# Moving eleven weight-conversion turns of a fused attention, gated-MLP and mixer kernel to earlier batches, with a new order in the last batch

## The chip, the cores and the metric

The kernel runs on one core of a Trainium2 chip. Its time is the device time of one execution in microseconds (us), taken as the median over several runs. One execution was also recorded by the hardware profiler, and all rows quoted below come from that one.

The engines have short names: PE is TensorE (matmuls), DVE is VectorE, ACT is ScalarE, POOL is GpSimd, and SP is SyncE, which here only issues DMA transfers.

## What is computed

Three layers follow one another, for a batch of 8, with 576 rows and 512 columns, all in float32:

```python
# attention: softmax of q over d, of k over s; no s x s matrix
q_s = softmax(q, axis=-1)
k_s = softmax(k, axis=2)
kv  = einsum('bhsd,bhse->bhde', k_s, v)
x   = einsum('bhsd,bhde->bhse', q_s, kv)          # heads joined to 512 columns
# gated MLP
u, v = split(gelu(x @ w_in))                       # 512 columns each
v_n  = (v - mean) / sqrt(var + 1e-6) * g_ln        # layer norm of v
v_s  = einsum('ts,bsd->btd', w_sg, v_n) + b_sg     # mixes the 576 rows
y    = x + (u * v_s) @ w_out
# mixer
u    = y + ((y^T @ U) @ V)^T                       # rank 32
out  = u + relu(u @ w_ch1) @ w_ch2                 # 512 -> 2048 -> 512
```

## The kernel before, in words

**Precision.** Nearly every matmul is made of three products of a high and a low part (`prod`, matmuls at L52). So each operand is split first: a rounding copy to the high part (L61, on ACT) and a subtraction that leaves the low part (L55, on DVE or POOL).

**Two phases.** The first phase is a loop over the eight batches. In this text b counts from 0, so b = 1 to 6 are batches 2 to 7 and b = 7 is the last. The 576 rows are four tiles of 128 and a short one of 64. The second phase is the channel MLP, over all batches at once in groups of rows: a long run of matmuls named `mm` that read weights `wu` back from a DRAM scratch `wd`.

**One batch has five stages.** In the V stage, `emit_Vh` makes the v half of `x @ w_in` tile by tile (`pv`), ACT applies the GELU, and DVE takes the row statistics (`stats`, L644 to L646). `emit_ln` then scales by the norm on ACT (L657) and splits. Beside it run the transposes, the rank-32 products and `emit_PV` of the batch before; `emit_PV` is the matmul `pw`, added into `yt` on DVE. In the U stage, `emit_Uh(b, f)` for f = 0 to 3 makes the u half (`pu`), and ACT turns each `pu` into `ut` with a GELU (L688). Beside it the next batch's softmax begins: DVE subtracts the row maximum (`q_sub`, `k_sub`), ACT takes exponentials (`q_exp` L483, `k_exp` L464). In the S stage, `emit_S(b, f)` makes the row mix (`pS`), DVE gates it (L708 and a multiplication by `ut`; that of f = 2 is done by POOL, by the table `GATES_POOL`), and `split_G` splits it into `gh` and `gl`. The y stage has the next batch's `kv` and transposed q (`pt`, split into `qh` on ACT and `ql` on DVE) and `emit_y(b, c)` (`py`), evicted into `yt` on DVE. The x stage makes the next `x`. The last batch has no next one; in its place the first products of the channel MLP (`pm`) run, on parts of u prepared by the steps of `prep` (`us`, `uh`, `ul`; loaded from the DRAM copy `u2d`).

**PSUM.** The tiles `pw`, `pu`, `pS`, `pt` of q and `py` share one pool of three buffers (tag `big`, `ps2`). Each takes the buffer of the third one before it, and so waits for whoever reads that one last. `pS` of f = 2 takes over from `pu` of f = 3, and waits for ACT's `ut` of f = 3. `py` of c = 1 takes over from the first `pt`, and waits for its `ql`. The last `pt` of q takes over from `py` of c = 1, and waits for its `yt`.

**Conversion turns.** The weights of the channel MLP are also split and summed before they are used. That work is cut into turns. The table `TURNS` lays 127 of them into the batches (per batch and stage, a string per slot; each `T` is a turn), `STEP_TURNS` 16 into the last batch's steps with `pm`, and `GROUP_TURNS` the rest into the second phase. `more(1)` does one turn: load the raw block (SP, L213, `stg`), clamp it (POOL, L171), take its rounding exponent (ACT, L177), merge (DVE, L183 and L184), add factor sums, write the high copy (`chw`, ACT, L61) and the low part (`chw`, POOL or DVE, L55), store to `wd` (SP, L384).

**What sets the order.** PE follows program order. DVE follows program order in the whole loop, since the loop body sits in `in_order(dve)`. The order on ACT, POOL and SP is chosen by the scheduler, by when it reckons each operation's input to be ready. Changing the place of an operation on DVE can therefore change the order on ACT too.

ACT holds one set of functions at a time. Going from exponentials to GELU or back takes an instruction of its own, `ACT_TABLE_LOAD`.

Of the kernel before, what the change touches and what calls it, by code (L numbers as in the profile page):

```python
# [22 lines left out]
def fused_kernel(tc, q, k, v, w_in, g_ln, w_sgT, b_sg, w_out, U, V, w_ch1, w_ch2, outT):  # L23
# [295 lines left out]
    GATES_POOL = ((), (2,), (2,), (2,), (2,), (2,), (2,), (2,))  # L319
# [3 lines left out]
    class Block(Conv):  # L323
# [14 lines left out]
        def high(self):  # L338
            pass
# [380 lines left out]
    y_t = {}  # L720

    def emit_y(b, c):
# [94 lines left out]
    def u_parts(g, kc):  # L817
# [6 lines left out]
        else:  # L824
            parts = [wrk.tile([P, F], F32, tag=x, name="us") for x in ("vh2", "vl2", "vh3", "vl3")]
# [10 lines left out]
    def u_first():  # L836
# [4 lines left out]
        for kc in range(2):  # L841
# [28 lines left out]
            if kc:  # L870
# [8 lines left out]
                high(5, u22)  # L879
                yield  # L880
                rest(5, u22)
                yield
                rest(4, u21)
                yield
# [331 lines left out]
    def in_order(*engines):  # L1216
# [107 lines left out]
    for b in range(B):  # L1324
# [13 lines left out]
        for t in range(NT + 1):  # L1338
            emit_Vh(b, t)
            if nxt:  # L1340
                with behind(dve):
                    for t2 in Q_MAX[b > 0][t]:
                        q_max(nxt, t2)
                    for _ in range(FOLDS[b > 0][t]):
                        next(fold)
            if t < NT:
                stats(b, t)
            slot(TURNS[b][0][t])
            if t > 0:
                emit_ln(b, t - 1)  # L1350
            if t == NT:
                stats(b, t)
            if b > 0:
                for t2 in ((2,), (3, 4), (), (), ())[t]:
                    emit_yT(b - 1, t2)
# [262 lines left out]
```

## Time and profile before

| | us |
|---|---|
| median of 3 runs | 1293.57 (1293.42 to 1298.71) |
| the profiled execution, its own time | 1292.16 |
| its span, first to last instruction | 1290.4 |
| PE busy | 1261.8 (98%) |
| DVE busy | 969.8 (75%) |
| ACT busy | 653.3 (51%) |
| POOL busy | 324.3 (25%) |
| mean granted TensorE clock | 0.989 of full speed |

The time is 1.8 us longer than the span, for what lies before the first and after the last instruction. Busy shares are averages over the program; stretches differ, and the stretch is what a change of a stage must be read from. In a row of a timeline, the first number is the start, the second the time from the start of the first to the end of the last of the instructions joined in it; the bracket at its end is how long the engine sat idle before and who ended that.

### The profile page before, as it was taken

What the parts mean: (1) busy time and instruction counts of PE and PEld (TensorE: products, weight loads), DVE (VectorE), ACT (ScalarE), POOL (GpSimd) and SP (SyncE); (2) the same over time, 40 slices, a digit from 0 to 9 for tenths busy, and PEclk for the clock granted to TensorE, in tenths of its full rate; (3) what the DMA queues carried; (4) which work ended last, traced back from release to release, by engine and by line L of the source; (5) the groups of instructions that cost most, each with busy time, mean ns of one, the idle gap of its engine ahead of it and who ended that gap; (6) DMA issues with size and microseconds to landing.
All of it is one profiled execution on the core that took longest, in us unless ns stands there. A gap on an engine that the chain in (4) does not pass through costs nothing.

```text
span 1290.4 us, 20684 instructions
## 1 busy us (share of the span) xinstructions
PE 1261.8 (98%) x7628; PEld 1142.8 (89%) x7628; DVE 969.8 (75%) x1406; ACT 653.3 (51%) x998; POOL 324.3 (25%) x421
## 2 busy tenths in 40 slices
PE   6999999999999999999999999999999999999998
PEld 5798999999998989797887888888888889999998
DVE  6898889797988888788769943597347953694485
ACT  5756667675757576754563512443224522451342
POOL 4734152623333334663630202000200002000000
PEclk8899999999999999999999999999999999999999
DMA  8515161715343352568998676678766788898786
GB/s 271 167 55 167 51 207 51 235 51 167 99 158 117 113 170 76 195 202 284 397 346 295 213 257 235 220 246 281 259 189 224 256 286 303 274 314 302 256 297 212
DMA packets 135909, 274.17 MB, mean 212 GB/s; under 512 B 15232, under 2 KB 56704, under 8 KB 135808
## 3 DMA queue, kind: packets, MB, share of 16 engines
q1 hardware_dynamic: 135808, 272.84, 64.0%
q8 instruction: 61, 1.00, 0.3%
q14 instruction: 40, 0.33, 0.1%
HBM read 224.56 MB, written 48.23 MB: 211 GB/s over the span
## 4 chain that ended last, share of the span: by engine, by line
PE 82%; DVE 8%; DMA 4%; ACT 3%; issue 1%; POOL 1%; SPq 1%; DVEq 0%; POOLq 0%; ACTq 0%
PE mm L52 51%; PE pS L52 8%; PE py L52 6%; PE pv L52 5%; PE pu L52 5%; PE px L52 1%; PE pk L52 1%; PE pt L553 1%; PE pt L741 1%; PE pp L52 1%; DVE bst L644 1%; DVE sh L654 1%; DMA wu<-wd 1%; DVE yt L55 1%; PE pm L52 1%
## 5 line engine op out<-in xcount | busy, mean ns | idle before, releaser
L52 PE MATMUL mm<-oh,wu 128*128 128x512 f32 (+1 forms) x1120 | 320.5, 367 | 1.2 <-DMA wu<-wd 1.2
L52 PE MATMUL mm<-uh,wu 128*128 128x512 f32 (+1 forms) x1064 | 303.4, 366 | 0.0
L52 PEld LDWEIGHTS mm<-oh,wu 128*128 128x128 f32 x1120 | 207.1, 188 | 27.6 <-ACT oh L61 1.6
L52 PEld LDWEIGHTS mm<-uh,wu 128*128 128x128 f32 x1064 | 196.6, 188 | 24.1 <-issue 0.2
L52 PE MATMUL mm<-ol,wu 128*128 128x512 f32 (+1 forms) x560 | 205.5, 367 | 0.0
L61 ACT ACTIVATE oh<-h 128x1024 fp32r<-128x1024 f32 (+1 forms) x140 | 135.2, 973 | 125.3 <-PE mm L52 104.6
L52 PE MATMUL mm<-ul,wu 128*128 128x512 f32 (+1 forms) x532 | 194.7, 366 | 0.0
L55 DVE TENSOR_TENSOR ol<-h,oh 128x1024 fp32r<-128x1024 f32 (+1 forms) x140 | 156.4, 1121 | 40.1 <-ACT oh L61 37.2
L55 POOL TENSOR_TENSOR ust<-ust 128x1024 f32<-128x1024 f32 (+1 forms) x16 | 36.3, 2278 | 384.5 <-DMA ust<-u2d 323.6
L55 DVE TENSOR_TENSOR h<-mm,u 128x1024 f32<-128x1024 f32 (+1 forms) x57 | 63.3, 1111 | 83.8 <-PE mm L52 83.8
L52 PEld LDWEIGHTS mm<-ol,wu 128*128 128x128 f32 x560 | 105.1, 188 | 13.2
L55 DVE TENSOR_TENSOR u<-mm,u 128x1024 f32<-128x1024 f32 (+1 forms) x53 | 58.9, 1111 | 73.2 <-PE mm L52 68.1
L52 PEld LDWEIGHTS mm<-ul,wu 128*128 128x128 f32 x532 | 99.9, 188 | 12.1
L55 POOL TENSOR_TENSOR chw<-f,chw 128x256 fp32r<-128x256 f32 x98 | 80.7, 836 | 97.6 <-ACT chw L61 87.6
L55 DVE TENSOR_TENSOR h<-h,h 128x1024 f32<-128x1024 f32 (+1 forms) x80 | 88.9, 1111 | 0.1
L1102 ACT ACTIVATE h<-mm 128x1024 f32<-128x1024 f32 (+1 forms) x19 | 17.8, 938 | 128.3 <-PE mm L52 128.3
L1093 ACT ACTIVATE h<-h 128x1024 f32<-128x1024 f32 (+1 forms) x60 | 58.1, 969 | 33.6 <-DVE h L55 33.6
L61 ACT ACTIVATE chw<-f 128x256 fp32r<-128x256 f32 x112 | 42.5, 411 | 63.6 <-DVE f L184 30.7
L61 ACT ACTIVATE u<-mm 128x1024 f32<-128x1024 f32 (+1 forms) x24 | 22.5, 936 | 96.3 <-PE mm L52 80.0
L171 POOL TENSOR_SCALAR stg<-stg 128x256 f32<-128x256 f32 (+1 forms) x88 | 44.3, 508 | 91.3 <-DMA stg<-in_w_ch_dram 50.4
L52 PE MATMUL pu<-xh,wih 128*128 128x288 f32 x256 | 57.9, 308 | 1.9 <-ACT wih L61 0.6
L52 PE MATMUL pu<-xh,wil 128*128 128x288 f32 x256 | 56.3, 301 | 1.8 <-DVE wil L55 1.8
(177 smaller groups left out, 2661.8 us busy)
## 6 DMA issues: line engine op xcount, KB each, us to landing
wu<-wd SPq DMA_DIRECT2D x280, 512.0 KB, 4.4
wd<-chw SPq DMA_DIRECT2D x112, 256.0 KB, 3.5
stg<-in_w_ch_dram SPq DMA_DIRECT2D x64, 256.0 KB, 3.5
u2d<-yt SPq DMA_DIRECT2D x32, 288.0 KB, 2.3
vt<-in_v_dram SPq DMA_DIRECT2D x32, 256.0 KB, 6.9
qt<-in_q_dram SPq DMA_DIRECT2D x7, 1024.0 KB, 8.2
kt<-in_k_dram SPq DMA_DIRECT2D x7, 1024.0 KB, 6.4
res<-u2d SPq DMA_DIRECT2D x12, 512.0 KB, 5.8
```

Of the source, the lines that this page charges most:

```text
L52: pe.matmul(out, lhsT, rhs, start=first, stop=last, skip_group_check=onto)
L55: return eng.tensor_tensor(out=out, in0=a, in1=b, op=op)
L61: return act.activation(out, src, AF.Copy)
L171: eng.tensor_scalar(out=hi, in0=hi, scalar1=F64_MOST, scalar2=-F64_MOST, op0=ALU.min, op1=ALU.max)
L553: pe.transpose(pt[:, t * P : (t + 1) * P], qt[:, t, c * P : (c + 1) * P], ident)
L644: dve.bn_stats(out=bst[0:n], in_=ge[0:n])
L654: dve.scalar_tensor_tensor(out=shift[0:n], in0=mv[0:n, 0:1], scalar=-1.0, in1=mv[0:n, 1:2], op0=ALU.mult, op1=ALU.mult)
L741: pe.transpose(pt[0:n, c * P : (c + 1) * P], y_t[b][:, c, t * P : t * P + n], ident)
L1093: act.activation(h, h, AF.Relu)
L1102: act.activation(h_out(j, 11, n), bank, AF.Relu)
```

## The change

It has four parts.

1. `TURNS`: 11 turns leave the last batch (29 to 18) and go to b = 1 to 4. Within those batches further turns go from the y stage to the S stage: the S stages of b = 1, 2, 3, 4 had 7, 6, 8 and 6 turns and have 12, 12, 11 and 9; the y stages had 8, 10, 6 and 8 and have 7, 7, 7 and 8. The sum over the batches stays 127, and the steps and the second phase have the turns they had.
2. In b = 1 to 6, two `q_sub` are put between the scaling and the split of the short tile's norm. They were the first after it.
3. The last batch: `emit_PV` and the low-rank copy come ahead of `stats` in the V stage, the short tile's norm and the `prep` steps are placed anew, its S stage has no turns, all gate multiplications are on DVE, `emit_y` for c = 0 and 1 runs jointly (f = 0 to 2 of both, then f = 3 of both), one scratch buffer is another, and some slots come after the added products.
4. In the last batch ACT follows program order too, from the U stage to the end of the y stage.

```diff
-    GATES_POOL = ((), (2,), (2,), (2,), (2,), (2,), (2,), (2,))
+    GATES_POOL = ((), (2,), (2,), (2,), (2,), (2,), (2,), ())
...
-        py = ps2.tile([P, 2, 512], F32, tag="big", name="py")
-        cs = slice(c * P, (c + 1) * P)
-        for fc in range(NF):
-            prod(py, wo_h[:, fc, cs], wo_l[:, fc, cs], gh[:, fc], gl2[:, fc], fc == 0, fc == NF - 1)
+        cols = (c,) if b < B - 1 or c > 1 else (0, 1)
+        if c == cols[0]:
+            for x in cols:
+                py_t[x] = ps2.tile([P, 2, 512], F32, tag="big", name="py")
+            for fcs in (range(NF - 1), range(NF - 1, NF)):
+                for x in cols:
+                    cs = slice(x * P, (x + 1) * P)
+                    for fc in fcs:
+                        prod(py_t[x], wo_h[:, fc, cs], wo_l[:, fc, cs], gh[:, fc], gl2[:, fc], fc == 0, fc == NF - 1)
+        py = py_t.pop(c)
...
-        (('T', '', '', '', ''), ('', '', '', ''), ('T', 'T', 'TTT', 'TT'), ('TT', 'TTTT', 'TTW', ''), ('', '', '', '', '')),
+        (('T', '', '', '', ''), ('', '', '', ''), ('TTT', 'TTTT', 'TTTT', 'T'), ('TT', 'TTT', 'TTW', ''), ('', '', '', '', '')),
...
-        (('TTT', 'TT', 'TT', 'T', 'TT'), ('TT', 'T', 'T', 'TTT'), ('TT', 'T', 'TT', ''), ('TTT', 'TT', 'PT', 'T')),
+        (('TTT', 'TT', 'TT', '', 'TTT'), ('T', 'T', '', ''), ('', '', '', ''), ('TT', 'TT', 'PT', 'T')),
...
+        else:
+            for t in range(NT + 1):
+                emit_Vh(b, t)
+                if t == 2:
+                    for t2 in range(NT + 1):
+                        emit_U(b - 1, t2)
+                for c in ((), (), (), (0, 1), (2, 3))[t]:
+                    emit_PV(b - 1, c)
                 stats(b, t)
+                if t >= NT - 1:
+                    emit_ln(b, t - 1)
+                slot(TURNS[b][0][t])
+                if 0 < t < NT - 1:
+                    emit_ln(b, t - 1)
...
+            acts = in_order(act)
+            acts.__enter__()
...
                 if b and nxt:
-                    emit_ln(b, NT)
+                    ln_scale(b, NT)
+                    for t in Q_SUB[1][0]:
+                        q_sub(nxt, t)
+                    ln_split(b, NT)
```

Three places where the order of instructions changes follow. The first is ACT in the U stage of b = 5, from the scaling of the short tile (L657, 64 rows) to the last `ut`. `qt` and `kt` are the next batch's exponentials, `vh` of 64 rows is the short tile's high copy. Before:

```order
L657 ACTIVATE ge<-ge,sh,mv 64x512
L61 ACTIVATE vh_5089<-ge 64x512
L688 ACTIVATE ut<-pu 128x576 x2
L483 ACT_TABLE_LOAD
L483 ACTIVATE qt<-qt 128x512 x4
L688 ACT_TABLE_LOAD
L688 ACTIVATE ut<-pu 128x576
L483 ACT_TABLE_LOAD
L483 ACTIVATE qt<-qt 64x512
L464 ACTIVATE kt<-kt 128x512 x4
L688 ACT_TABLE_LOAD
L688 ACTIVATE ut<-pu 128x576
```

And now, from the table load behind the same scaling:

```order
L483 ACT_TABLE_LOAD
L483 ACTIVATE qt<-qt 128x512
L61 ACTIVATE vh_5149<-ge 64x512
L483 ACTIVATE qt<-qt 128x512
L688 ACT_TABLE_LOAD
L688 ACTIVATE ut<-pu 128x576 x2
L483 ACT_TABLE_LOAD
L483 ACTIVATE qt<-qt 128x512 x2
L483 ACTIVATE qt<-qt 64x512
L464 ACTIVATE kt<-kt 128x512
L688 ACT_TABLE_LOAD
L688 ACTIVATE ut<-pu 128x576
```

```order
L464 ACT_TABLE_LOAD
L464 ACTIVATE kt<-kt 128x512 x4
L61 ACTIVATE chw<-f_4732 128x256
L61 ACTIVATE chw<-f_4714 128x256
L688 ACT_TABLE_LOAD
L688 ACTIVATE ut<-pu 128x576
```

The first exponentials moved ahead of the first two `ut`: six table loads and all ten exponentials now come before the last `ut`, where four loads and nine exponentials stood. Each of b = 1 to 6 has this order; the two `chw` copies ahead of the last load are there in b = 5 only.

The second is DVE at the end of the S stage of b = 3, from the last gating (L708) to the first two `ql`. Before:

```order
L708 SCALAR_TENSOR_TENSOR gt<-pS,gl,bb 128x576
L55 TENSOR_TENSOR gt<-gt,ut 128x576
L55 TENSOR_TENSOR gl_3518<-gt,gh 128x576 x2
L183 TENSOR_SCALAR f_3650<-f_3650 128x256
L184 SCALAR_TENSOR_TENSOR f_3650<-stg,f_3650 128x256
L55 TENSOR_TENSOR ql<-pt,qh 128x576 x2
```

And now:

```order
L708 SCALAR_TENSOR_TENSOR gt<-pS,gl,bb 128x576
L55 TENSOR_TENSOR gt<-gt,ut 128x576
L55 TENSOR_TENSOR gl_3558<-gt,gh 128x576 x2
L55 TENSOR_TENSOR chw<-f_2994,chw 128x256
L183 TENSOR_SCALAR f_3692<-f_3692 128x256
L184 SCALAR_TENSOR_TENSOR f_3692<-stg,f_3692 128x256
L183 TENSOR_SCALAR f_3701<-f_3701 128x256
L184 SCALAR_TENSOR_TENSOR f_3701<-stg,f_3701 128x256
L55 TENSOR_TENSOR ql<-pt,qh 128x576 x2
```

One merge stood between `gl` and `ql`; now a low part and two merges do.

The third is DVE in the V stage of the last batch, from the low-rank copy `pst` to the first additions of `emit_PV`. Before:

```order
L55 TENSOR_TENSOR pst<-pp,pst 32x512
L644 BN_STATS bst<-ge 128x6
L645 BN_AGGR mv<-bst 128x2
L646 TENSOR_SCALAR mv<-mv 128x1
L183 TENSOR_SCALAR f_6710<-f_6710 128x256
L184 SCALAR_TENSOR_TENSOR f_6710<-stg,f_6710 128x256
L654 SCALAR_TENSOR_TENSOR sh<-mv 128x1
L55 TENSOR_TENSOR yt<-pw,yt 128x576 x2
```

And now:

```order
L55 TENSOR_TENSOR pst<-pp,pst 32x512
L644 BN_STATS bst<-ge 128x6
L645 BN_AGGR mv<-bst 128x2
L646 TENSOR_SCALAR mv<-mv 128x1
L183 TENSOR_SCALAR f_6707<-f_6707 128x256
L184 SCALAR_TENSOR_TENSOR f_6707<-stg,f_6707 128x256
L183 TENSOR_SCALAR f_6716<-f_6716 128x256
L184 SCALAR_TENSOR_TENSOR f_6716<-stg,f_6716 128x256
L654 SCALAR_TENSOR_TENSOR sh<-mv 128x1
L55 TENSOR_TENSOR yt<-pw,yt 128x576 x2
```

The statistics and the two merges that now follow `pst` stood just ahead of it before. The additions now stand ahead of the next tile's statistics and merge, which they followed.

## Rows read from the trace of the kernel before

**Rows 1.** The page, part 1: busy time, share and instructions of each engine.
```profile
PE 1261.8 (98%) x7628; PEld 1142.8 (89%) x7628; DVE 969.8 (75%) x1406; ACT 653.3 (51%) x998; POOL 324.3 (25%) x421
```

**Rows 2.** Windows by stage: us, busy time per engine, PEclk, DMA share, GB/s.
```profile
382.80:451.50 68.70, 68.49 (x532) 64.61 (x531) 59.96 (x110) 44.34 (x74) 24.19 (x36) 1.00 0.39 126
...
520.20:613.00 92.80, 88.87 (x540) 79.07 (x539) 76.85 (x129) 53.15 (x105) 50.01 (x63) 1.00 0.67 222
613.00:686.00 73.00, 71.82 (x317) 59.23 (x317) 52.34 (x64) 39.93 (x65) 35.33 (x49) 1.00 1.01 375
```

**Rows 3.** Timeline of ACT, U stage of b = 5: start, us, instruction, idle before.
```profile
409.64 0.82 ACT L657 ACTIVATE ge<-ge,sh,mv 64x512 f32<-64x512 f32 x1 [1.50 <-DVE sh L654]
...
411.70 1.20 ACT L688 ACTIVATE ut<-pu 128x576 f32<-128x576 f32 x2 [0.58 <-DMA u2d<-yt]
412.91 1.28 ACT L483 ACT_TABLE_LOAD   x1
414.21 2.19 ACT L483 ACTIVATE qt<-qt 128x512 f32<-128x512 f32 x4
...
423.70 0.65 ACT L688 ACTIVATE ut<-pu 128x576 f32<-128x576 f32 x1
...
426.21 0.71 ACT L61 ACTIVATE chw<-f 128x256 fp32r<-128x256 f32 x2
```

**Rows 4.** Timeline of PE, the same stretch: the start of `pS` for f = 2.
```profile
425.91 0.42 PE L52 MATMUL pS<-sg_h,vh 128*128 128x288 f32 x2
```

**Rows 5.** Timeline of DVE, S to y stage of b = 3.
```profile
293.91 1.65 DVE L55 TENSOR_TENSOR chw<-f,chw 128x256 fp32r<-128x256 f32 x1
...
296.13 0.42 DVE L55 TENSOR_TENSOR chw<-f,chw 128x256 fp32r<-128x256 f32 x1
...
299.32 1.64 DVE L55 TENSOR_TENSOR gl<-gt,gh 128x576 fp32r<-128x576 f32 x2
300.88 0.28 DVE L183 TENSOR_SCALAR f<-f 128x256 uint32<-128x256 uint32 x1
...
301.54 1.42 DVE L55 TENSOR_TENSOR ql<-pt,qh 128x576 fp32r<-128x576 f32 x2
```

**Rows 6.** Timeline of PE, the same stretch: the start of `py` for c = 1.
```profile
302.94 0.43 PE L52 MATMUL py<-gh,wo_h 128*128 128x288 f32 x2
```

**Rows 7.** Timelines of DVE, POOL and PE, y stage of b = 1.
```profile
169.01 0.76 DVE L55 TENSOR_TENSOR yt<-py,x 128x576 f32<-128x576 f32 x1 [1.41 <-PE py L52]
...
168.99 1.45 POOL L55 TENSOR_TENSOR chw<-f,chw 128x256 fp32r<-128x256 f32 x2
...
172.54 0.71 PE L553 MATMUL pt<-ident,qt 128*128 128x128 f32 x5
```

**Rows 8.** Timeline of PE in the last batch, V to U stage.
```profile
539.05 0.80 PE L52 MATMUL pw<-v_w,pst 128*128 128x288 f32 x4 [0.26 <-DVE pst L55]
...
541.55 0.43 PE L52 MATMUL pw<-v_w,pst 128*128 128x288 f32 x2
543.27 0.53 PE L52 MATMUL pw<-v_w,pst 128*128 128x288 f32 x2 [1.29 <-DVE yt L55]
543.94 0.54 PE L52 MATMUL pu<-xh,wih 128*128 128x288 f32 x2
...
547.85 0.53 PE L52 MATMUL pu<-xh,wih 128*128 128x288 f32 x2 [0.46 <-DVE yt L55]
```

**Rows 9.** Waits of PE from 519 to 690 us: total us, times, longest us.
```profile
PE pw L52 <- DVE yt L55: 1.7, 2, 1.3
PE mm L52 <- DMA wu<-wd: 1.2, 1, 1.2
PE pm L52 <- ACT h L1102: 0.8, 1, 0.8
PE py L52 <- DVE gl L55: 0.5, 1, 0.5
```

**Rows 10.** Timeline of ACT in the last batch: its third part of u.
```profile
550.89 0.64 ACT L61 ACTIVATE uh<-us 128x512 fp32r<-128x512 f32 x1 [0.63 <-DMA us<-u2d]
```

More of the change, by code (lines that the diff above doesn't have):

```diff
@@ L720, in fused_kernel @@
     y_t = {}
+    py_t = {}
     def emit_y(b, c):
@@ L824, in u_parts @@
         else:
-            parts = [wrk.tile([P, F], F32, tag=x, name="us") for x in ("vh2", "vl2", "vh3", "vl3")]
+            parts = [wrk.tile([P, F], F32, tag=x, name="us") for x in ("vh2", "vl2", "vh3", "vh4")]
         parts = [t[:, 0:n] for t in parts]
@@ L878, in u_first @@
                 tt(dve, u22, u22, u11, ALU.subtract)
-                high(5, u22)
-                yield
-                rest(5, u22)
                 yield
                 rest(4, u21)
+                yield
+                high(5, u22)
+                rest(5, u22)
                 yield
@@ L1337, in fused_kernel @@
             load_ahead()
[L1338 to L1346, printed above, removed]
-                stats(b, t)
[L1348 to L1353, printed above, removed]
+        if nxt:
+            for t in range(NT + 1):
+                emit_Vh(b, t)
+                if nxt:
+                    with behind(dve):
+                        for t2 in Q_MAX[b > 0][t]:
+                            q_max(nxt, t2)
+                        for _ in range(FOLDS[b > 0][t]):
+                            next(fold)
+                if t < NT:
+                    stats(b, t)
+                slot(TURNS[b][0][t])
+                if t > 0:
+                    emit_ln(b, t - 1)
+                if t == NT:
+                    stats(b, t)
+                if b > 0:
+                    for t2 in ((2,), (3, 4), (), (), ())[t]:
+                        emit_yT(b - 1, t2)
+                if t == 2 and b > 0:
+                    for t2 in range(NT + 1):
+                        emit_U(b - 1, t2)
+                if b > 0:
+                    for c in ((), (), (), (0, 1), (2, 3))[t]:
+                        emit_PV(b - 1, c)
+        else:
+            for t in range(NT + 1):
+                emit_Vh(b, t)
+                if t == 2:
+                    for t2 in range(NT + 1):
+                        emit_U(b - 1, t2)
+                for c in ((), (), (), (0, 1), (2, 3))[t]:
+                    emit_PV(b - 1, c)
+                stats(b, t)
+                if t >= NT - 1:
+                    emit_ln(b, t - 1)
+                slot(TURNS[b][0][t])
+                if 0 < t < NT - 1:
+                    emit_ln(b, t - 1)
                 for t2 in ((2,), (3, 4), (), (), ())[t]:
                     emit_yT(b - 1, t2)
-            if t == 2 and b > 0:
-                for t2 in range(NT + 1):
-                    emit_U(b - 1, t2)
-            if b > 0:
-                for c in ((), (), (), (0, 1), (2, 3))[t]:
-                    emit_PV(b - 1, c)
         spread_at = 2 if b else 3
@@ L1384, in fused_kernel @@
             if not nxt:
-                for _ in range((0, 3, 3, 3)[f]):
+                for _ in range((0, 1, 3, 3)[f]):
                     next(prep, None)
@@ L1403, in fused_kernel @@
             if nxt:
-                for t in Q_SUB[b > 0][f]:
+                for t in Q_SUB[b > 0][f] if b == 0 or f else ():
                     q_sub(nxt, t, pool if t in Q_SUB_POOL[b > 0] else dve)
@@ L1413, in fused_kernel @@
                         k_sub(nxt, t)
-            if not nxt and f == 1:
+            if not nxt and f == 2:
                 ln_split(b, NT)
@@ L1417, in fused_kernel @@
                 slot(TURNS[b][1][f])
-            if not nxt and f == 0:
+            if not nxt and f == 1:
                 ln_scale(b, NT)
@@ L1439, in fused_kernel @@
         for f in range(NF):
+            if not nxt:
+                for _ in range((5, 0, 0, 0)[f]):
+                    next(prep, None)
             emit_S(b, f)
@@ L1447, in fused_kernel @@
                     k_exp(nxt, ((0, 1, 2), (3, 4))[f])
-            if not nxt:
-                for _ in range((2, 0, 0, 0)[f]):
-                    next(prep, None)
             if f > 0:
@@ L1457, in fused_kernel @@
             with tc.issue_after(last['s'].ins):
-                for _ in range(2):
+                for _ in range(1):
                     next(prep, None)
@@ L1504, in step @@
                 after(s)
-                for _ in range((1, 0, 9, 0, 0, 0, 0)[s]):
+                for _ in range((1, 0, 0, 0, 0, 0, 0)[s]):
                     next(prep, None)
-                slot(STEP_TURNS[s])
+                if s < 4:
+                    slot(STEP_TURNS[s])
             pvl = ((), (), (), (), (0, 1), (2,), (3,))
@@ L1526, in fused_kernel @@
                 pvs(s)
-                for _ in range(2 if s == 1 else 0):
+                for _ in range((0, 2, 9, 0, 0, 0, 0)[s]):
                     next(prep, None)
+                if s >= 4:
+                    slot(STEP_TURNS[s])
         gate.clear()
```

2 lines of the change are left out of this document (added), and 5 rows, old and new, of the table TURNS.

## The prediction, made before the result was known

> **What bounds the kernel now.** I read the busy shares first [rows 1]: PE has 98%, the next engine 75%. A time can then only change where PE starts late, so the second view is the table of windows [rows 2]. In b = 5, which stands for b = 1 to 6 (six windows of 68.6 to 68.8 us), PE is busy 68.49 of 68.70 us: there is next to nothing to win in these batches, only to lose. The last batch has 3.9 us without PE in 92.8. The stretch behind it has 1.2 in 73, with the DMA engines full (share 1.01).
>
> The third view is PE's waits from 519 us on [rows 9]. Its four largest kinds are 4.2 us in five waits, and two more of 0.26 and 0.46 stand in the timeline [rows 8]: 4.9 in seven. A wait costs a little more than its length, because the pipeline fills again: a pair of these matmuls steps on by 0.27 (0.43 for a pair, less the 0.16 by which the pairs overlap), so after 541.55 the next was due at 541.82 and came at 543.27, 1.45 late for a wait of 1.29. With 0.16 for each of the seven, and 0.4 more at the pair after that (0.67 to 543.94 in place of 0.27 [rows 8]), **6.4 us is all that this change can win**: 0.49% of the time. What a measurement of this kernel can tell from no change is about 0.5%, or 6.47 us. So a measurable gain is nearly excluded before any part is costed. The question is what the parts lose.
>
> **Part 1, the two subtractions in the short tile's norm: a loss of 7.0.** The subtractions themselves only swap places on DVE. But they are done earlier, and so ACT's order turns over: exponentials now come ahead of the first two `ut`, and six table loads instead of four ahead of the last. I lay ACT's new order out with the old durations. In b = 5 the scaling of the short tile ends at 409.64 + 0.82 = 410.46 [rows 3]. Behind it stand:
> - six table loads of 1.28, with a gap of 0.02 each (412.91 + 1.28 to 414.21): 7.8;
> - ten exponentials at 2.19 / 4 = 0.55: 5.5;
> - the short tile's copy, at the price of one of two `ut` (1.20 less 0.65): 0.55;
> - four `ut`, 1.20 for two and 0.65 for each of the others: 2.5.
>
> That is 16.35, so the last `ut` ends at 426.8. It ended at 424.35 before (423.70 + 0.65). `pS` of f = 2 needs the buffer that it frees, and started at 425.91 [rows 4]: what was a slack of 1.5 becomes a wait of 0.9, and 0.15 of refill makes 1.05. The order and the durations repeat in b = 1 to 6, so six times 1.05 is 6.3. In b = 5 two high copies stand ahead of the last load besides, 0.71 [rows 3]. **Sum 7.0.** PE has no slack behind it in which this could come back. The wait of the first `ut` for a DMA (0.58 [rows 3]) doesn't add: the load that now comes first isn't held by it, and 0.58 is over by then. DVE's low part of the short tile waits for a later copy, some 1.8 us; that is work PE needs only at the end of the first `pS`, so it costs nothing while `pS` is itself late.
>
> Bounds of this part: at least 4, if unlike instructions overlap by half a microsecond more per batch than the sum has it; at most 9.5, if ACT also waits for DVE's subtractions 0.4 per batch.
>
> **Part 2, the added turns: a loss of 2.2.** Each adds a clamp, an exponent, a merge of 0.7 (300.88 to 301.54 [rows 5]), copies, lows and DMAs. DVE is busy 60 of 68.7 us and the DMA share is 0.39 [rows 2], so the engines have the room; only the place counts. SP's and POOL's queues get up to five turns more within an S stage; POOL is busy 24 of 68.7 and loses nothing but order.
> - In b = 3, a low part and a second merge come between `gl` and the first `ql`. A low part took 0.42 alone and 1.65 beside POOL [rows 5], which are DVE's bounds for it; I take 0.42 for want of a POOL operation there. With the merge that is 1.1. ACT's order too puts the last `gh` behind the first two `qh`, which wait for PE's transposes; I reckon that this holds `gl` back by 1.9: two copies go ahead of it, at a `ut`'s 0.6 each [rows 3], and the transposes that they wait for come with PE's own delay of 1.05, of which 0.7 tells (they were done a little before they were asked for). `ql` ended at 302.96 in pair, its first half at 302.25; `py` of c = 1 started at 302.94 [rows 6], a slack of 0.7. With 3.0 more for `ql`, and 1.05 more for `py` by PE's own delay, 1.3 is left: **1.4** with the refill. Bounds 0 (if `gh` goes first in time after all) and 2.6 (the low part at its slow price).
> - In b = 1, three merges stand between the first and second `yt`, and their exponents on ACT are behind a `qh` and a POOL low part (1.45 for two [rows 7]). The second `yt` ended at 169.77; the last transposes, which need its buffer, started at 172.54 [rows 7], so 2.8 of slack. Three merges are 2.1, the POOL pair 1.45, two exponents 0.4 each (as half of the two copies of 0.71 [rows 3]): 4.4, against 2.8 of slack and 1.05 of PE's delay. That leaves 0.6, with refill **0.8**; bounds 0 and 1.7, as the exponents find POOL free or held up twice.
> - In b = 2 and b = 4 what comes between the same pairs is no more than one merge, which the slack of 0.7 and PE's delay cover: 0. Without this cover it would be 0.7 each at the most, which I leave to the range.
>
> **Part 3, the last batch: a gain of 4.2.** The copy `pst` and the additions of `emit_PV` stood on DVE behind statistics and merges. Now they stand ahead. PE's starts came late at four places there: 0.42 before 539.05 and 0.62 before 547.85 (their waits and refill), 1.45 before 543.27 and 0.4 before 543.94 [rows 8]: 2.9 together, which I count as won in full, since the engines that were waited for had other work in front that is now behind. The joint `emit_y` puts the first three f of c = 1 between the last gate and the first use of its `gl`: that wait of 0.5 [rows 9] goes, 0.7 with refill. Of the wait of `pm` for ACT (0.8) and the second of `pw` (0.4, the rest of 1.7 [rows 9]), which hang on work that starts earlier but stands in the same order, I count half: 0.6. The wait for `wu` (1.2 [rows 9]) stays: the DMA engines are full there [rows 2] and must move the same bytes. Bounds 2.5 and 5.5.
>
> **The sum.** 7.0 + 1.4 + 0.8 - 4.2 = +5.0. The profiled execution took 1292.16, and would take 1297.2; the median is 1.4 above the profiled one, so the time shown for the changed kernel should be 1293.57 + 5.0 = **1298.6**. By its own bounds it lies between 1294 and 1303.
>
> **What the Trainium skill says of it.** In this trace an exponential starts 0.02 us after a table load of 1.28 ends, and the load 0.01 after the `ut` before it [rows 3]: a switch costs 1.30 and no more. The Trainium skill, "ScalarE: Activation LUTs", section "What ACT_TABLE_LOAD costs", gives about 1283 ns for the load, which the trace has too, and a drain of about 1380 ns with it, 2.66 us for every switch. The trace here shows no such drain. By that rule the two added loads would cost 5.3 per batch and not 2.6, and the sum would be some 16 us higher.
>
> **The rivals.**
> - *The last batch gives nothing back* (slower). In the last batch ACT now keeps the written order, and two `uh`, which wait for the loads of u from DRAM, stand ahead of the second `ut`. `pS` of f = 0 needs that `ut`, and is due 2.9 us earlier than before, at about 554.6. The third such part was ready at 550.89 before [rows 10]; if ACT reaches the `ut` as that one ends, it is done at 552.2, with 2.4 to spare. The point from which this decides: loads that land over 2.4 us later than they did. For it: the DMA engines serve stores and weight loads in the same stretch. Against it: the turns there went away, 11 of them, and their transfers with them. Then the 2.9 are lost again: +7.9, **1301.5**.
> - *ACT isn't late* (faster, or none). If the last `ut` were done by 425.9, 0.9 earlier than my sum, part 1 would cost nothing but b = 5's copies, and part 2 nothing that isn't covered. Only the gain of part 3 is left: 1293.57 - 4.2 + 0.7, **1290**. For it: the sum has single gaps taken from other neighbours, and the wait is small against 16 us. [...]
> - *Both, and all of PE's waits go:* -6.4, **1287**. Against it: the wait for `wu`, on full DMA engines.
> - *A table load drains as well* (slower). If each of the two added loads held ACT for as long again as its 1.28 [rows 3], `pS` of f = 2 would wait 2.6 more in each of six batches: +15.4, **1314**. It is the mechanism of the Trainium skill's rule above. Against it: the gaps of 0.01 and 0.02.
>
> **How the numbers follow.** My forecast gets 0.62: it rests on ACT's order and on durations that repeat. The last batch giving nothing back gets 0.17, ACT not late 0.16, all waits gone 0.03, the drain 0.02. The range from **1290** to **1304** takes in the forecast with its bounds, the first rival with the upper bound of part 2, and the 1290 of the second; what it leaves out is half of the second, the two last ones, and the ends of the bounds: under 0.2. Slower by over 0.5% means above 1300.04: the first rival with 0.13 of its 0.17, the drain, and a fourth of the forecast, together 0.31. Faster by over 0.5% means below 1287.1: 0.03. The rest, 0.66, is within 0.5%. The forecast itself lies at +0.39%, on the slow side of no change.
>
> **What would show it.** In the changed profile's waits of PE, a line for `pS` released by ACT at L688, six times, about 1 us each and longest in b = 5; the windows of b = 1 to 6 each some 1.1 longer with the same busy PE time; a wait of `py` for DVE's `ql` in b = 3. In the last batch, no wait of `pw` for `yt`, and a stage shorter by 4. I am wrong if `pS` shows no wait for ACT, if the last batch isn't shorter, or if PE waits at another place for over 2 us.

## The result, and the profile after

| | before | changed |
|---|---|---|
| median of the runs, us | 1294.55 (1293.42 to 1298.71, 6 runs) | 1305.36 (1301.12 to 1306.31, 6 runs) |
| ratio, 95% interval | | 1.0072 (1.0052 to 1.0093) |
| profiled execution: span, us | 1290.4 | 1299.3 |

The change makes the kernel slower by 0.72%, some 9.3 us: the ratio is that of the means (1295.2 and 1304.6); the medians lie 10.8 apart. The profiled execution of the changed kernel is the fastest of its six, and its first 130 us took 1.05 less (first `pu` of b = 1 at 129.13, before at 130.18), with a higher granted clock there (0.92 against 0.87 in the first 108 us). From that `pu` on it is 10.0 us longer. That is the difference to explain, and it is laid out by stage here. From here on the parts are numbered as in the prediction: part 1 is the two subtractions in the short tile's norm, part 2 the turns (the list of the change has these two the other way round), parts 3 and 4 the last batch's new order and ACT's program order there. A stage is measured on PE, from its first matmul to the first of the next stage (`pu` for U, `pS` for S, `pk` for y, `px` for x, `pv` for V).

| us longer than before | U and S | y | x and V |
|---|---|---|---|
| b = 1 | 0.98 | 1.80 | 1.25 |
| b = 2 | 1.15 | 0.86 | 0.0 |
| b = 3 | 1.15 | 2.22 | 0.0 |
| b = 4 | 0.98 | 0.61 | 0.30 |
| b = 5 | 1.74 | 0.15 | 0.09 |
| b = 6 (up to `px`) | 1.16 | 0.41 | 0.0 |
| sum | 7.2 | 6.1 | 1.6 |

The last batch is shorter: 2.4 in V, 0.8 in U, 0 in S, 1.3 in y with its first products, and 0.4 in the second phase: 4.8 in sum, before rounding. 7.17 + 6.06 + 1.61 - 4.84 = 10.0.

The page's first part stands against [rows 1]: PE is as busy as before in a longer span.

```profile
PE 1261.5 (97%) x7628; PEld 1137.3 (88%) x7628; DVE 966.0 (74%) x1407; ACT 651.9 (50%) x998; POOL 318.5 (25%) x420
```

The view that says most is PE's waits in the changed kernel from 100 to 700 us (us in total, times, longest). Before, the wait for `yt` by `pw` and that for `wu` led this list [rows 9]; both are gone from this stretch, and four kinds that had no line there stand at its head.

```profile
PE pS L52 <- ACT ut L688: 4.1, 6, 1.2
PE pt L553 <- DVE yt L55: 1.6, 2, 1.4
PE py L52 <- DVE ql L55: 1.5, 2, 1.2
PE px L52 <- DVE xl L55: 1.0, 2, 0.8
...
PE py L52 <- DVE gt L708: 0.5, 1, 0.5
```

**Part 1: ACT's order.** ACT's timeline in the U stage of b = 1, to be read against [rows 3]. Its first row is the scaling of the short tile, which ended at 134.76.

```profile
133.95 0.81 ACT L657 ACTIVATE ge<-ge,sh,mv 64x512 f32<-64x512 f32 x1 [1.50 <-DVE sh L654]
...
136.62 0.61 ACT L61 ACTIVATE vh<-ge 64x512 fp32r<-64x512 f32 x1
137.14 0.62 ACT L483 ACTIVATE qt<-qt 128x512 f32<-128x512 f32 x1
137.78 1.28 ACT L688 ACT_TABLE_LOAD   x1
139.07 1.19 ACT L688 ACTIVATE ut<-pu 128x576 f32<-128x576 f32 x2
...
145.75 1.28 ACT L464 ACT_TABLE_LOAD   x1
147.05 2.19 ACT L464 ACTIVATE kt<-kt 128x512 f32<-128x512 f32 x4
149.26 1.28 ACT L688 ACT_TABLE_LOAD   x1
150.55 0.65 ACT L688 ACTIVATE ut<-pu 128x576 f32<-128x576 f32 x1
```

The last `ut` ends at 151.20, 16.4 after the scaling; the prediction's sum had 16.35. A load is followed by its first function 0.02 later (145.75 + 1.28 to 147.05), as before. PE in the same stretch: `pS` of f = 2 starts 0.76 late. Before that `pu` of f = 3 had come 0.22 late, since the first `ut` was late as well; the U stages of b = 1 to 6 are 0.3 longer each, 1.9 of the 7.2.

```profile
150.23 0.43 PE L52 MATMUL pS<-sg_b,vh 128*128 128x288 f32 x2
151.26 0.53 PE L52 MATMUL pS<-sg_h,vh 128*128 128x288 f32 x2 [0.59 <-ACT ut L688]
```

**Part 2: turns at the head of a queue.** In b = 3, what DVE does from the end of its S stage (against [rows 5]):

```profile
304.06 0.94 DVE L55 TENSOR_TENSOR chw<-f,chw 128x256 fp32r<-128x256 f32 x1 [3.51 <-POOL f L55]
...
305.58 0.81 DVE L708 SCALAR_TENSOR_TENSOR gt<-pS,gl,bb 128x576 f32<-128x576 f32 x1
...
310.37 1.41 DVE L55 TENSOR_TENSOR ql<-pt,qh 128x576 fp32r<-128x576 f32 x2
```

A low part of a turn waits 3.51 us for a factor sum on POOL. The gating of the last `pS`, which PE had finished at 302.32, stands behind it. So both the first `py` and the second come late (PE, against [rows 6]):

```profile
306.54 0.49 PE L52 MATMUL py<-gh,wo_h 128*128 128x288 f32 x2 [0.49 <-DVE gt L708]
...
311.17 0.53 PE L52 MATMUL py<-gh,wo_h 128*128 128x288 f32 x2 [1.22 <-DVE ql L55]
```

In b = 1 (against [rows 7]) the second `yt`, which ended at 169.77 before, starts at 173.25. It stands on DVE behind merges, one of which waits 1.10 for its exponent on ACT. That exponent stands on ACT behind `qh` and a turn's high copy, and the copy waits 1.20 for a sum on POOL. The rows are DVE's, ACT's, and PE's.

```profile
171.23 0.35 DVE L183 TENSOR_SCALAR f<-f 128x256 uint32<-128x256 uint32 x1 [1.10 <-ACT f L177]
...
173.25 0.75 DVE L55 TENSOR_TENSOR yt<-py,x 128x576 f32<-128x576 f32 x1
```
```profile
169.88 0.42 ACT L61 ACTIVATE chw<-f 128x256 fp32r<-128x256 f32 x1 [1.20 <-POOL f L55]
...
170.76 0.44 ACT L177 ACTIVATE f<-stg 128x256 f32<-128x256 f32 x1
```
```profile
174.06 0.76 PE L553 MATMUL pt<-ident,qt 128*128 128x128 f32 x5 [1.42 <-DVE yt L55]
```

The x stage of b = 1 shows the same on ACT: two high copies wait 2.67 for sums on POOL, `xh` stands behind them, and PE's `px` waits 0.83 for the `xl` that is made from it.

```profile
179.18 0.72 ACT L61 ACTIVATE chw<-f 128x256 fp32r<-128x256 f32 x2 [2.67 <-POOL f L55]
```

**Part 3: the last batch.** PE's two `pw` pairs and the `pu` behind them follow without a wait, where [rows 8] had four late starts.

```profile
552.43 0.69 PE L52 MATMUL pw<-v_w,pst 128*128 128x288 f32 x4
...
554.81 0.69 PE L52 MATMUL pw<-v_w,pst 128*128 128x288 f32 x4
555.34 0.43 PE L52 MATMUL pu<-xh,wih 128*128 128x288 f32 x2
```

### The profile page after: what moved, and what is told of

Same layout as the page of the kernel before. It is cut to its first block, busy times and chain, and to the rows that moved or that the text cites. A ratio compares the mean times of both kernels' runs of the same rounds, so it can differ in the third digit from the quotient of the medians.

```text
span 1299.3 us, 20690 instructions
## 1 busy us (share of the span) xinstructions
PE 1261.5 (97%) x7628; PEld 1137.3 (88%) x7628; DVE 966.0 (74%) x1407; ACT 651.9 (50%) x998; POOL 318.5 (25%) x420
## 4 chain that ended last, share of the span: by engine, by line
PE 70%; DVE 10%; ACT 8%; DMA 5%; issue 4%; POOL 3%; SPq 0%; DVEq 0%; ACTq 0%; POOLq 0%
PE mm L52 51%; PE pv L52 6%; PE py L52 3%; PE pS L52 2%; DMA stg<-in_w_ch_dram 2%; PE px L52 2%; PE pm L52 1%; ACT L688 1%; PE pp L52 1%; PE pt L748 1%; DVE f L183 1%; PE pu L52 1%; ACT qt L483 1%; POOL chw L55 1%; DVE yt L55 1%
## 5 line engine op out<-in xcount | busy, mean ns | idle before, releaser
L52 PE MATMUL py<-gh,wo_h 128*128 128x288 f32 x256 | 57.0, 304 | 4.6 <-DVE gt L708 2.1
L52 PE MATMUL pS<-sg_h,vh 128*128 128x288 f32 x256 | 55.6, 298 | 4.1 <-ACT ut L688 4.1
```

Source lines behind the costliest of these rows:

```text
L52: pe.matmul(out, lhsT, rhs, start=first, stop=last, skip_group_check=onto)
```

## The experiments

Ratios are against the kernel before, run beside each on the same chip. Stage times are from the one profiled execution of each kernel, in us longer than before.

**1 to 4: the parts apart.** Four kernels: without part 1, with part 1 alone, with the new table of turns alone, with parts 3 and 4 alone.

```diff
# e1: the changed kernel
-                    ln_scale(b, NT)
-                    for t in Q_SUB[1][0]:
-                        q_sub(nxt, t)
-                    ln_split(b, NT)
+                    emit_ln(b, NT)
...
-                for t in Q_SUB[b > 0][f] if b == 0 or f else ():
+                for t in Q_SUB[b > 0][f]:
# e2: the kernel before, the same lines the other way round
# e3: the kernel before, with the changed kernel's TURNS
# e4: e1, with the TURNS of the kernel before
```

> The changed kernel with part 1 undone: the two subtractions stand behind the short tile's norm again. Theory: the wait of pS (f = 2) for ACT's last ut goes in all of b = 1 to 6, and the first ut is in time for pu (f = 3); these two cost 7.2 us in the changed kernel (U and S stages of b = 1 to 6 longer by 0.98, 1.15, 1.15, 0.98, 1.74, 1.16), so this run should lie 7.2 below the changed kernel, about +2.8 us against the kernel before, if the parts add up. Rival, cover: PE's delay of 1 us in each S stage also gave the conversion work on DVE and ACT 1 us more before PE's y stage asked for it; without it each of the y stages of b = 1 to 4 loses up to 1 us more, and the run lies only 3.2 below the changed kernel, about +6.8.

> The kernel before with part 1 alone. Theory: six waits of pS (f = 2) for ut at L688, 0.75 us each (1.0 of lost time with the pu before it), y stages unchanged: +6 to +7 us against the kernel before. Rival: the wait needs the turns as well (ACT's order is set by all its work), and part 1 alone costs under 2 us.

> The kernel before with the new table of turns alone (11 turns from the last batch to b = 1 to 4, others from y to S). Theory: no wait of pS for ut; y stages of b = 1, 2, 3, 4 longer by what the changed kernel shows there, 3.05, 0.8, 2.2 and 0.9 (with the stages behind them), 7 in sum, less what the last batch wins by having 11 turns fewer (0 to 1.5): +5.5 to +7 us. Rival, cover: the same stages lose up to 1 us more each without PE's delay ahead of them, +9 to +11. Second rival: the turns cost nothing by themselves (it was part 1's delay that put them in the wrong place), 0 to +1.

> The kernel before with parts 3 and 4 alone (the last batch's new order, ACT in program order there), the turns where they were, all 29 of the last batch among them. Theory: the gain lies in the order: V stage of the last batch shorter by 2.4, U by 0.8, y with its steps by 1.3, the wait for wu by 0.3, together -4.8 us. Rival: the gain needs the 11 turns gone, whose merges otherwise stand in DVE's and ACT's written order ahead of what PE asks for: -1 to -2.5.

| | ratio (interval) | U, S of b = 1 to 6 | y of b = 1 to 6 | x, V of b = 1 to 5 | last batch on |
|---|---|---|---|---|---|
| all parts | 1.0072 (1.0052 to 1.0093) | 7.2 | 6.1 | 1.6 | -4.8 |
| e1, parts 2 to 4 | 1.0028 (1.0015 to 1.0041) | 0.1 | 6.4 | 3.7 | -2.3 |
| e2, part 1 | 1.0070 (1.0055 to 1.0086) | 7.3 | 0.6 | 3.4 | +1.0 |
| e3, part 2 | 1.0055 (1.0039 to 1.0072) | 0.0 | 4.9 | 2.7 | -1.2 |
| e4, parts 3 and 4 | 1.0022 (1.0008 to 1.0037) | 0.0 | 0.0 | 0.0 | +0.5 |

Part 1 does by itself what was said of it: 7.3 in the U and S stages, and none of it where it is left out. The parts do not add up, though. Part 1 costs 9 us alone, more than the 6 to 7 expected, and 5.7 with the others (1.0072 less 1.0028). The cover that the first rival named is there in two stages: without PE's delay of 1 us the y stage of b = 1 loses 3.7 and not 1.8, that of b = 3 2.7 and not 2.2. But b = 2 and 4 lose nothing without that delay, and 0.9 and 0.6 with it, so that over all y stages the cover is worth 0.3 and is not the reason. In the traces the difference lies in the x and V stages and from the last batch on; why is open.

e1, at +3.6 us, lies nearer to the 2.8 of its theory than to the 6.8 of its rival. e3, at +7, lies at the top of its theory: the turns cost by themselves, and not only behind part 1's delay. e4 went as its rival had it, and worse: the new order alone wins 3.2 in the V and U stages, and loses 4.5 in the y stage, because the turns of the S stage stand on DVE ahead of the last gating, and one of them waits there for POOL. DVE's, POOL's and PE's rows there:

```profile
572.29 0.93 DVE L55 TENSOR_TENSOR f<-f,f 128x256 f32<-128x256 f32 x1 [1.00 <-POOL chw L55]
573.14 0.80 DVE L708 SCALAR_TENSOR_TENSOR gt<-pS,gl,bb 128x576 f32<-128x576 f32 x1
```
```profile
571.52 1.42 POOL L55 TENSOR_TENSOR chw<-f,chw 128x256 fp32r<-128x256 f32 x2
```
```profile
575.46 0.85 PE L52 MATMUL py<-gl,wo_h 128*128 128x288 f32 x2 [3.06 <-DVE gl L55]
```

Its profiled execution, 1291.58, was the lowest of twelve (median 1297.63), so the ratio says more than this trace. Parts 3 and 4 were always run together; what ACT's program order (part 4) does by itself is not shown.

Three of the four traces show a loss that no theory had: V stages of single batches longer by 1 to 2, in e1 (b = 1 and 2), e2 (b = 1 and 5) and e3 (b = 1). In e2 that of b = 1 is 1.9 longer. SP issues the load of the next q at 176.69, 5.1 before the V stage; before it did so at 173.27, 7.3 ahead. DVE's row maxima then wait, and a low part of y, which PE's `pv` waits for, stands behind them. SP's row and DVE's row of e2, then SP's of the kernel before:

```profile
176.69 0.38 SPq L133 DMA_DIRECT2D qt<-in_q_dram  x1
```
```profile
186.43 1.87 DVE L474 TENSOR_REDUCE qm<-qt 128x8 f32<-128x512 f32 x3 [2.73 <-DMA qt<-in_q_dram]
```
```profile
173.27 0.38 SPq L133 DMA_DIRECT2D qt<-in_q_dram  x1
```

**5: ACT's order alone.** DVE's order stays exactly that of the changed kernel.

```diff
# e5: the changed kernel
-            with contextlib.nullcontext() if b else tc.issue_after(last['g', 3].ins):
+            with tc.issue_after(last['g', 1 if b else 3].ins):
                 for t in range(NT + 1):
                     q_exp(nxt, t)
```

> The changed kernel, DVE's order exactly as it is there, with the next batch's exponentials held until the second ut is done: on ACT the short tile's copy and two ut come first again, and four table loads and ten exponentials stand ahead of the last ut in place of six loads and ten. Theory (ACT's order alone makes part 1's cost): the last ut ends 13.8 us after the short tile's scaling, pS (f = 2) has 1.6 of slack, its six waits go, and the run lies as far below the changed kernel as the run with part 1 undone does, 5 to 7 us, about +0.3% against the kernel before. Rival (DVE's place of the two subtractions costs by itself, since the short tile's low part waits behind them): pS of f = 0 to 2 or the gates stay late, and under half of it comes back.

Measured 1.0035 (1.0020 to 1.0050), 4.8 us below the changed kernel: a little under the 5 to 7 of the theory, and over the half that the rival set. The U and S stages of b = 1 to 6 are as before to 0.03 us each; the windows of these two stages in b = 1, of e5 and then of the changed kernel:

```profile
131.68:145.30 13.62, 13.53 (x103) 13.29 (x101) 13.18 (x23) 10.94 (x16) 3.09 (x3) 1.00 0.25 88
145.30:160.31 15.01, 15.01 (x115) 14.84 (x113) 12.62 (x27) 8.17 (x13) 2.12 (x4) 1.00 0.22 71
```
```profile
129.13:143.05 13.92, 13.79 (x103) 13.32 (x102) 11.68 (x21) 11.52 (x16) 3.09 (x3) 1.00 0.25 86
143.05:158.73 15.68, 15.09 (x114) 14.69 (x112) 14.20 (x29) 10.05 (x15) 1.83 (x4) 1.00 0.22 66
```

So the place of the two subtractions on DVE costs nothing there; the order that follows from it on ACT, with its two added table loads, is the whole cost of part 1 in these stages. What is left lies mostly in the turns. The V stage of b = 1 is 4.5 longer, and ACT shows a third way in which a turn gets there: a high copy waits for the store that frees its buffer, and `xh`, which PE's `pv` needs, stands behind it. The same wait is there in e1 (0.46) and e3 (1.28).

```profile
186.25 0.42 ACT L61 ACTIVATE chw<-f 128x256 fp32r<-128x256 f32 x1 [2.45 <-DMA wd<-chw]
186.91 0.42 ACT L61 ACTIVATE chw<-f 128x256 fp32r<-128x256 f32 x1 [0.24 <-DMA wd<-chw]
187.23 0.63 ACT L61 ACTIVATE xh<-px 128x576 fp32r<-128x576 f32 x1
```

**6: turns where the traces showed no loss.**

```diff
# e6: e1, rows b = 1 and 3 of TURNS as before, and
-        (('', '', '', '', ''), ('', 'B', 'T', 'T'), ('', 'TB', 'TTT', 'TT'), ('T', 'TT', 'TT', 'T'), ('', '', '', '', '')),
+        (('', '', '', '', ''), ('', 'B', 'T', 'T'), ('T', 'TTB', 'TTTT', 'TT'), ('T', 'TT', 'TT', 'T'), ('', '', '', '', '')),
...
-        (('TTT', 'TT', 'TT', '', 'TTT'), ('T', 'T', '', ''), ('', '', '', ''), ('TT', 'TT', 'PT', 'T')),
+        (('TTT', 'TT', 'TT', '', 'TTT'), ('TT', 'TT', 'T', ''), ('', '', '', ''), ('TT', 'TT', 'PT', 'T')),
```

> A version made from what the runs showed: part 1 undone, parts 3 and 4 kept, and the turns placed where the traces showed no loss: b = 1 and 3 as in the kernel before, b = 2 and 4 as in the changed one, three more in the S stage of b = 5, and 21 of the 29 in the last batch, none in its S stage. Theory (the losses are single turn operations in the y stages of b = 1 and 3 and the late loads of q; the last batch's order gains 4.5 once its S stage holds no turns): y stages of b = 1 to 4 as before, last batch shorter by 3.5 to 4.5, no wait of pS: -2 to -4.5 us, 0.997 to 0.9985. Rival: the turns cost wherever they are put (each needs 2 us of DVE, ACT and POOL), so what the last batch wins is lost in b = 2, 4 and 5: 0 to +3 us.

Measured 1.0026 (1.0011 to 1.0040): the rival. b = 1 lost nothing again, but b = 2, which had lost nothing in e1 with the very same row of the table, lost 4.0 in its y stage, and b = 6, untouched, 2.3. A turn's operations are spread over later slots, and so a row of the table means something else behind other rows. A place without loss is not a property of that place.

**7: two low parts off DVE in b = 3.**

```diff
# e7: e1
-    DVE_FACTOR_LOWS = {5: (1, 3, 5, 7), 4: (1, 3, 4), 3: (3, 7), 2: (1, 3)}
+    DVE_FACTOR_LOWS = {5: (1, 3, 5, 7), 4: (1, 3, 4), 2: (1, 3)}
```

> The kernel with part 1 undone, where in b = 3 the two factor low parts on DVE (chw, L55) are given to POOL; everything else on DVE stays in its order. There the y stage of b = 3 was 2.65 us longer than before: py (c = 0) waits 0.9 for the last gating, which stands on DVE behind a low part that waits for a sum on POOL, and py (c = 1) 1.2 for ql. Theory (a turn's operation that waits at the head of DVE's queue): the first wait goes, the second shrinks by the 0.4 of the other low part, and the y stage of b = 3 is 1.2 to 1.6 longer than before, no more. Rival (DVE's plain time, as I had reckoned in the prediction): only the two durations go, 0.4 to 0.8 in all, and the wait for the gating stays.

Measured 1.0020 (1.0006 to 1.0035). The y stage of b = 3 is 1.7 longer than before in place of 2.7. PE's wait for the gating (0.9 in e1) has no line any more; that for `ql` kept its 1.2, since `py` was due earlier by what the first wait had cost. That is a little above the range of the theory, and the wait that the rival said would stay is gone. The gating starts 1.0 after the first `pk` in place of 3.8 in e1, while the low part itself took 0.94 there: it is the wait at the head of DVE's queue, more than DVE's time.

**8: the load of q from another queue.**

```diff
# e8: e2, in load_q (both loads)
-            sp.dma_start(qt[:, t : t + step, :], src)
+            (act if b > 1 else sp).dma_start(qt[:, t : t + step, :], src)
```

> The kernel before with part 1 alone, where the loads of q for b = 2 and later are issued from ACT's queue in place of SP's. In the run with part 1 alone, the V stage of b = 1 was 1.9 longer and that of b = 5 1.2: the row maxima of q on DVE waited 2.7 for a load of q that SP had issued 5.1 us before the V stage and not 7.3, behind stores that wait for low parts; PE's pv then waited for a low part of y behind those maxima on DVE. Theory (SP's queue order makes the load late): the load leaves as soon as the last transposes of q are done, no wait of DVE for q, the V stages of b = 1 to 6 at 18.3 as in the kernel before; 1 to 3 us below the run with part 1 alone. Rival (the DMA engines are what is late, whoever issues): the same waits stay.

Measured 1.0085 (1.0060 to 1.0109), no better than e2. In b = 1 the load leaves 6.8 before the V stage and not 5.1, and DVE's wait is 1.56 and not 2.73: the queue's order had its part. That load takes 10.2 from ACT's queue, and took 9.7 from SP's both in e2 and in the kernel before. So what made it late in e2 was its issue, 2.2 later against the V stage, and not a longer transfer. In the x stage of b = 0, though, PE waits 3.6 for `xl`: as a remedy it failed.

**9: the last batch's turns out of its S stage.**

```diff
# e9: e4, with another last row of TURNS
-        (('TTT', 'TT', 'TT', 'T', 'TT'), ('TT', 'T', 'T', 'TTT'), ('TT', 'T', 'TT', ''), ('TTT', 'TT', 'PT', 'T')),
+        (('TTT', 'TT', 'TT', 'T', 'TTT'), ('TT', 'T', 'T', 'T'), ('', '', '', ''), ('TTT', 'TTT', 'PTTT', 'TTTT')),
```

> The kernel before with parts 3 and 4 and all 29 turns of the last batch still in it, but none of them in its S stage and 5 in its U stage in place of 7: the V stage has 11 and the y stage 13 in place of 7; all other batches as before. With the turns where they stood, parts 3 and 4 won 3.2 in the V and U stages and lost 4.5 in the y stage, where py waited 4.4 for gl, the last gating of DVE's queue being behind a sum that waited for POOL. Theory (it is the operations ahead of the gatings in the S stage that cost, and not the number of turns in the batch): no wait of py for gl over 0.7, V and U stages shorter by 3.2, y stage within 1.5 of before: -1.5 to -4 us against the kernel before. Rival (29 turns are too many for this batch wherever they stand): the y stage or the first products wait as long as S did, 0 to +3 us.

Measured 0.9997 (0.9986 to 1.0008), the rival's side. V and U win 3.2 again, S loses nothing, and the y stage loses 3.6: its longest waits are for DVE now, in place of the 4.4 for `gl`.

```profile
PE pt L748 <- DVE yl L55: 2.0, 1, 2.0
PE py L52 <- DVE gl L55: 1.3, 1, 1.3
```

The operations ahead of the gating were what cost in e4, but 13 turns in y were too many for y.

**10: fewer table loads.**

```diff
# e10: the kernel before
-            with contextlib.nullcontext() if b else tc.issue_after(last['g', 3].ins):
+            with tc.issue_after(last['g', 3].ins):
                 for t in range(NT + 1):
                     q_exp(nxt, t)
-            if b:
-                k_exp(nxt)
+                if b:
+                    k_exp(nxt)
```

> The kernel before, where all exponentials of the next batch are held until the last ut is done: two table loads a batch in place of six. Theory (a table load costs PE nothing while the ut that it stands before has slack, 1.5 us here): U and S stages as before, 13.6 and 15.0; ACT's busy time falls by 24 loads of 1.28, 31 us; the time is the same within 0.2%, if the sums of the exponentials on DVE, 2.7 us later at most, do not reach the gatings of S. Rival (ACT's room matters as a whole: the copies of the turns and of xh come earlier when ACT has 5 us more a batch): 1 to 3 us faster.

Measured 1.0082 (1.0065 to 1.0098), outside both: slower. The U and S stages are as before and 24 table loads fewer were made (13, 12, 8 and 6 in four groups before, 7 and 8 now, beside the one at the start of both), yet the y stages of b = 1 to 6 are 1.0 to 2.6 longer each. DVE waits for the late exponentials, its sums and normalisation then hold the gatings, and the merges of the S stage come where `ql` is asked for (PE waits for it five times, 3.6 in all). DVE in b = 1:

```profile
147.69 3.05 DVE L489 TENSOR_REDUCE qs<-qt 128x8 f32<-128x512 f32 x5 [3.32 <-ACT qt L483]
...
151.38 3.04 DVE L55 TENSOR_TENSOR qt<-qt,qs 128x512 f32<-128x512 f32 x5
154.34 0.80 DVE L708 SCALAR_TENSOR_TENSOR gt<-pS,gl,bb 128x576 f32<-128x576 f32 x1
```

**11 and 12: between the two.** The same last row of the table, with 13, 8, 0 and 8 turns in V, U, S and y (e11: `('TTT', 'TTT', 'TTT', 'T', 'TTT'), ('TT', 'TT', 'TT', 'TT'), ('', '', '', ''), ('TT', 'TT', 'PTT', 'TT')`), and with 11, 9, 0 and 9 (e12: `('TTT', 'TT', 'TT', 'T', 'TTT'), ('TT', 'TT', 'TT', 'TTT'), ('', '', '', ''), ('TT', 'TTT', 'PTT', 'TT')`).

> The kernel before with parts 3 and 4, all 29 turns of the last batch in it: 13 in its V stage (before 10), 8 in U (7), none in S (5), 8 in y (7). With 13 in y the V and U stages won 3.2 and the y stage lost 3.6 to its merges, ahead of the transposes. Theory (only the places count, ahead of what PE asks for next): V and U stages shorter by 3.2, y stage by 0 to 1: -2.5 to -4.5 us against the kernel before, 0.9965 to 0.998. Rival (the last batch's DVE has no room for 29 turns, wherever they stand): what the y stage no longer loses is lost in V or U, where merges delay the norm and the parts of u; -1 to +2 us.

> The same with 11 turns in V, 9 in U, none in S, 9 in y. Theory: as the run with 13 in V, -2 to -4 us, with up to 1 us more in the y stage for its ninth turn. Rival: two turns more in U stand on DVE ahead of the parts of u and on ACT ahead of the third and fourth ut, and pS of f = 0 to 2 waits for ut: 0 to +2 us.

e11 measured 0.9979 (0.9965 to 0.9993), 2.7 us under the kernel before and inside its theory; it is the only one of these kernels whose whole interval lies below 1. Its last batch has V -2.2, U -0.7, S +0.5, y +0.2; its trace also has a V stage of b = 5 that is 1.6 longer, where no turn was moved. e12 measured 1.0006 (0.9993 to 1.0019): V and U win 3.5, but S loses 1.7 to gatings that come late and y 0.8. The two differ by two turns in V, one in U and one in y. Its rival had the right size by another wait: `pS` waited for the gating, 1.0, and for `ut` only 0.2.

```profile
PE pS L52 <- DVE gt L708: 1.0, 1, 1.0
...
PE pS L52 <- ACT ut L688: 0.2, 1, 0.2
```

## Why the prediction was right or wrong

The forecast was 1298.6, +5.0 us and within 0.5%; measured were +9.3, 0.72%. With this ratio the 1293.57 from which the forecast started becomes 1302.9, near the upper end of its range of 1290 to 1304. The sign and the mechanism of the largest term were right. That the time would stay within 0.5% was not; slower than that had been given 0.31.

- **Part 1: 7.0 predicted, 7.2 found** in the changed kernel and 7.3 alone. Its reading, that the cost lies in ACT's order and that six loads and ten exponentials put the last `ut` 16.35 after the scaling, is shown by the 16.4 in the trace and by e5, which changes that order alone. The sum put all of it at `pS` of f = 2; in fact 0.3 of each batch's loss comes earlier, at `pu` of f = 3, and `pS` is late by that much less. That PE has no slack to win it back held too.
- **Part 2: 2.2 predicted, 6.3 found**: 5.5 in the y stages of b = 1 to 4 and 0.8 in the x stage of b = 1. (The 0.6 in the y stages of b = 5 and 6 is there in e2 too, where no turn was moved, and the 0.8 left in x and V stages is not shown to be the turns' doing.) This is the step that failed. It reckoned a turn on DVE by its duration ("a low part and a second merge come between"), and only in b = 1 by what it waits for. The runs showed that a turn's operation blocks by its wait: 3.51 for a sum on POOL in b = 3, a chain from DVE over ACT to POOL in b = 1, and in e5 a store that has not landed. "POOL is busy 24 of 68.7 and loses nothing but order" was true and beside the point, since POOL's order is what the others wait for.
  - In b = 3, 1.4 stood against 2.2 (2.7 without part 1), and what was near in it was luck: 1.9 of its 3.0 was `gl` held back by two `qh` ahead of `gh` on ACT. In the trace ACT had done these and stood idle for 0.33 until DVE's gating came (first row below), so this cost nothing, and the low part that had been put at 0.42 cost its wait.
  - In b = 1, 0.8 stood against 1.8 in y and 0.8 in x. The chain was in the sum, at 4.4; counted from the first `pu`, the second `yt` ended 5.3 later than before.
  - b = 2 and 4 were put at 0, and lost 0.9 and 0.6; they lose nothing with either part alone (e2, e3). In b = 2 `qh` stood on ACT behind two high copies that waited 1.63 for a sum on POOL, DVE's `ql` waited for it (the other rows), and PE's `py` then waited 0.6 for a late `yt`.

```profile
307.22 0.69 ACT L61 ACTIVATE gh<-gt 128x576 fp32r<-128x576 f32 x1 [0.33 <-DVE gt L55]
```
```profile
238.23 0.73 ACT L61 ACTIVATE chw<-f 128x256 fp32r<-128x256 f32 x2 [1.63 <-POOL f L55]
```
```profile
239.52 0.76 DVE L55 TENSOR_TENSOR ql<-pt,qh 128x576 fp32r<-128x576 f32 x1 [1.64 <-ACT qh L61]
```

- **Part 3: 4.2 predicted, 4.8 found.** The 2.9 before `pS` came out as 3.2. The 0.7 of the joint `emit_y` was a misreading: PE still loses 0.67 at that place. The wait is for the low part of f = 2, the eighth pair of the first `py`, and the joint order moves f = 3 alone. The rows are PE's before and now. The rest of the gain came from the steps. That the wait for `wu` stays was wrong: at 685 us, where the kernel before waited 1.2, there is none, and 0.4 some 400 us later. But there is none at that place in e2 and e10 either, whose last batch is as before, so this is not shown to be the change's doing.

```profile
574.99 0.53 PE L52 MATMUL py<-gl,wo_h 128*128 128x288 f32 x2 [0.51 <-DVE gl L55]
```
```profile
585.58 0.53 PE L52 MATMUL py<-gl,wo_h 128*128 128x288 f32 x2 [0.51 <-DVE gl L55]
```

- **Not foreseen: part 3 needs the S stage of the last batch free of turns.** I costed parts 2 and 3 apart. e4 shows that the order alone is slower by 0.22%; with the five turns of that S stage placed elsewhere in the same batch it is 0.9997 (e9) and 0.9979 (e11). So no turn had to leave the batch: e11 keeps all 29, where sending eleven away cost more than the 4.8 that the last batch won.
- **The rivals.** That the last batch gives nothing back did not happen: the second `ut` was done 3.0 before `pS` asked for it. ACT was late, as forecast. With the drain that the Trainium skill, "ScalarE: Activation LUTs", section "What ACT_TABLE_LOAD costs", adds to every switch, the two added loads would be an estimated 5.3 a batch. The trace of the changed kernel doesn't agree: it again has 0.02 between a load and the function behind it, and the 16.4 fits without a drain.

## What to carry to other kernels

Before an operation is moved into an engine's fixed order, list what it waits for and not only how long it takes: behind it, the time that counts is that of the slowest engine in its chain. Where one engine's order is chosen by a scheduler, an edit on another engine can turn it over, so compare the orders of all engines, and count the function-table switches between the producer and the matmul that needs the buffer. Slack left by one change is used up by the next (b = 2 and 4 lost 0.9 and 0.6 in their y stages with parts 1 and 2 together, and nothing with either alone): price parts together, by the stage in which both end.

## What the runs showed of the hardware that was not expected

Fewer table loads made the kernel slower (e10, 1.0082 with 24 loads of 1.28 us fewer), since the function that the loads had brought early was what another engine's queue waited for. And the time of a 1 MB load of q from issue to landing differed by batch: 5.6 to 9.7 us in the kernel before, all from SP. That of b = 1 took 9.7 there, 9.7 in e2 from SP, and 10.2 in e8 from ACT's queue. Issued 7.3 ahead of the V stage, as before, it cost PE nothing; issued 5.1 ahead, as in e2, it made that stage 1.9 longer.
